# G in two stages, u of two batches in one tile, and v of batch 1 in pieces

## The chip, the cores and the metric

The kernel runs on one core of one Trainium2 chip. The metric is device time in microseconds; the times here are in microseconds unless a unit is named. The engines are PE (TensorE, with its weight loads listed apart as PEld), DVE (VectorE), ACT (ScalarE), POOL (GpSimd) and SP (SyncE, which here only issues transfers). Each works through its own list of instructions in order, and they wait for each other through semaphores.

## The reference

A landmark attention (Nystromformer) over 8 batches, 8 heads, 576 positions and 64 channels is followed by a multiplicative feed-forward layer. All inputs and the output are float32.

```python
q_lm, k_lm = means of q and k over 18 neighbouring positions      # 32 landmarks
A  = softmax(q @ k_lm.T / 8)      # 576 x 32
Bm = softmax(q_lm @ k_lm.T / 8)   # 32 x 32
C  = softmax(q_lm @ k.T / 8)      # 32 x 576
Z  = Bm.T / (norm(Bm, 1) * norm(Bm, inf) + 1e-6)
for _ in range(6):
    Z = 2 * Z - Z @ Bm @ Z
x  = A @ Z @ C @ v                # heads side by side: 4608 x 512
out = ((x @ w1) * (x @ w2)) @ w3 @ w_out
```

## The kernel before

The kernel never forms x. For each batch it makes `zt`, the 32 rows of Z @ C @ v of each head, multiplies them by w1 and w2 into `g` (tile `gt`), and has x @ w1 as `ahat` times `g`, where `ahat` holds the normalised A of four heads. w3 @ w_out is multiplied out once, at the start, into `w34`.

*Start (the fold).* The generator `fold` yields 64 products (L507, three matmuls each) that make `w34`; `turn` transposes blocks of w3 on PE ahead of them (L494). A row of w34 is summed in the PSUM tile `acc` and emptied by ACT (L510). The attention of batch 0 is interleaved with it: a loop over n takes one step of the attention and then one or two products.

*Attention.* The generator `attention` yields after each stage. In order: landmarks `lm` from `parts` (L201, L206) and `qbd`; Bm (psB, L217, then exponent and row sums); the scores C0 and C1 of four heads each (L242, exponent `ect` on ACT, presums on POOL, L253 and on); psR and A0 (L306, L292, exponent `eat`), A1 with the first product C @ v (L323, L328), the second product; six iterations it0 to it5 (L387), with the softmax denominators of A (L349) behind it1; psZ (L407), `zt` in two halves by ACT (L412) and DVE (L413), and `normalise(0)` (L371 on PE, `ahat` on DVE, L374); then `normalise(1)` and G. G has four blocks: two halves of the 1024 columns, each for w1 and w2. A block is 16 matmuls of 64x32 tiles (L430), and is emptied by ACT for w1 (L434) and by DVE for w2 (L436). They are called G00, G01, G10 and G11 here, by column half and matrix.

*Batches.* A loop over b runs the feed-forward part of batch b and, between its matmuls, the attention of batch b + 1. The up phase has 8 units j; each makes 128 columns of both products, 288 + 288 positions: `up(st, j, 0)` is four matmuls (L444) that ACT empties into `a_sb` (L448), `up(st, j, 1)` is four more that DVE multiplies with `a_sb` into `ab` (L450), this is u. Between the two stands one stage of the attention. Then the down phase multiplies `ab` by `w34` in chunks of 128 positions (L464), each in two halves of four matmuls; after each half comes one stage. ACT empties a chunk into `o_sb` (L470) and SP writes it out. As 576 is four and a half chunks, an odd batch begins with a split chunk: 64 positions of the batch before and 64 of its own, in eight 64-wide matmuls for each half. So even batches have 8 halves and odd ones 10. In an even batch two stages follow half n = 6.

At the end of a batch the first stage (L201, `lm`) of the attention after next is run, so that it begins ahead of the up phase.

*PSUM.* Three tiles `big` of two banks are shared by up, C, A, the iterations, the denominators (kept from it1 until `rmix`), normalise, G and every second chunk of down. `acc` and `small` are one bank each.

*Transfers.* POOL issues q and k, as one transfer per tensor (`load_qk`) or as pieces (`qk_pieces`, advanced from inside `landmarks`). SP issues v, the DMA transposes of q and k (`turn_all`, L106), w3, and the output. `load_v_piece` has ACT copy one element into the destination first, so that the transfer waits for ACT's place in its list; `load_v` has no such copy. The order on each engine is the one written in the program.

Of the kernel before, what the change touches and what calls it, by code (L numbers as in the profile page):

```python
# [8 lines left out]
FP16 = mybir.dt.float16  # L9
# [6 lines left out]
S = 576  # L16
# [9 lines left out]
NP = 96  # L26
# [5 lines left out]
def kernel(  # L32
# [42 lines left out]
    def load_v(st, b):  # L75
        vt = st["vt"] if "vt" in st else pin.tile([128, H, 384], FP32, name="vt")
        nc.sync.dma_start(out=vt[0:NP], in_=v[b].rearrange("h (p r) d -> p h (r d)", p=NP))
        st["vt"] = vt
# [117 lines left out]
    def attention(st, bank=None):  # L196
# [225 lines left out]
        for n in range(2):  # L422
            for w in range(2):
                psG = big()
                fs = slice(512 * n, 512 * n + 512)
                for i in range(2):
                    for h in range(4):
                        for qd in range(2):
                            rs = slice(64 * qd, 64 * qd + 64)
                            nc.tensor.matmul(psG[32 * h:32 * h + 32, qd, :], zt[rs, i, h, :],  # L430
                                             wup[rs, h, w, fs], start=(i == 0), stop=(i == 1),
                                             tile_position=(64 * qd, 32 * h))
                if w == 0:
                    nc.scalar.activation(out=g[:, :, w, fs], in_=psG, func=AXF.Copy, scale=1.0 / ZS)  # L434
                else:
                    nc.vector.tensor_scalar(out=g[:, :, w, fs], in0=psG, scalar1=1.0 / ZS,  # L436
                                            scalar2=None, op0=ALU.mult)
                yield

    def up(st, j, w):  # L440
        p = big()
        for qd in range(2):
            for c in range(2):
                nc.tensor.matmul(p[:, c, 0:HS], st["g"][:, qd, w, 128 * j:128 * j + 128],  # L444
                                 st["ahat"][qd][:, c, :], start=(qd == 0), stop=(qd == 1))
        if w == 0:
            st["a_sb"] = po.tile([128, 2, HS], FP16, name="a_sb", bufs=2)
            nc.scalar.copy(out=st["a_sb"], in_=p[:, :, 0:HS])  # L448
        else:
            nc.vector.tensor_tensor(  # L450
                out=st["ab"][:, j, :].rearrange("p (c s) -> p c s", c=2),
                in0=st["a_sb"], in1=p[:, :, 0:HS], op=ALU.mult)


    rows = out.rearrange("(b p g) f -> b g p f", b=B, g=6)

    def down(srcs, half, hold, bank):
        if half == 0:
            hold["ps"] = bank()
        pso = hold["ps"]  # L460
        for j in range(4 * half, 4 * half + 4):
            o = 0
            for _, ab, s0, sz in srcs:
                nc.tensor.matmul(pso[o:o + sz, :], ab[:, j, s0:s0 + sz], w34[:, j, :],  # L464
                                 start=(j == 0), stop=(j == 7),
                                 tile_position=(0, o))
                o += sz
        if half == 1:
            o_sb = po.tile([128, DM], FP32, name="o_sb")
            nc.scalar.activation(out=o_sb, in_=pso[:, :], func=AXF.Copy,  # L470
                                 scale=1.0 / (X64 * X64))
            o = 0
            for b, _, s0, sz in srcs:
                while sz:
                    gi, p0 = divmod(s0, NP)
                    n = min(sz, NP - p0)
                    nc.sync.dma_start(out=rows[b, 2 * (gi % 3) + gi // 3, p0:p0 + n, :],
                                      in_=o_sb[o:o + n, :])
                    o, s0, sz = o + n, s0 + n, sz - n


    def fold(pf, wof, w3f, wsp, warm_up):
# [58 lines left out]
    with tc.tile_pool(name="pf", bufs=2) as pf:  # L541
        wof, w3f = {}, {}
        wsp = pf.tile([128, 2, 8, DM], FP16, name="wsp", bufs=1)

        def load_w3(j, cc=None, eng=nc.sync):
            if j not in w3f:
                w3f[j] = pf.tile([128, DF], FP32, name="w3f", bufs=3)
            sl = slice(0, DF) if cc is None else slice(512 * cc, 512 * cc + 512)
            eng.dma_start(out=w3f[j][:, sl], in_=moe_w3[128 * j:128 * (j + 1), sl])

        def load_wout(c, eng):
            wof[c] = pf.tile([128, DM], FP32, name="wof", bufs=6)
            eng.dma_start(out=wof[c], in_=moe_w_out[128 * c:128 * c + 128, :])

        load_w3(0, 0)
        load_wout(0, nc.scalar)
        load_wout(1, nc.sync)
        load_w3(1, 0, nc.scalar)
        load_wout(2, nc.sync)
        load_wout(3, nc.scalar)  # L560
        load_w3(0, 1)
        load_wout(4, nc.scalar)
        load_w3(1, 1)
        load_wout(5, nc.scalar)

        warm = pf.tile([128, 512], FP16, name="warm", bufs=1)
        nc.vector.memset(warm, 0.0)
        psw = big()

        def warm_up(n):  # L570
            for _ in range(n):
                nc.tensor.matmul(psw[:, 0, :], warm[:, 0:128], warm, start=True, stop=True)

        warm_up(7)

        nc.gpsimd.tensor_copy(out=gate, in_=wof[4][:, 0:1])
        load_qk(sts[0], 0)
        load_qk(sts[1], 1)
        load_weight(0, moe_w1)
        load_weight(1, moe_w2)  # L580
        mask4, par, ones, eye2, iit, onesq, selc, lomask = constants()
        fd = fold(pf, wof, w3f, wsp, warm_up)
        steps(fd, 1)
        load_wout(6, nc.sync)
        load_wout(7, nc.sync)
        load_w3(2)
        steps(fd, 7)
        load_w3(3)
        steps(fd, 8)
        w3f[4] = pf.tile([128, DF], FP32, name="w3f", bufs=3)  # L590
        nc.gpsimd.tensor_copy(out=w3f[4][0:NP, 0:1], in_=sts[0]["qkn"][0:NP, 1, 0, 0:1])
        load_w3(4)
        sts[0]["vt"] = pin.tile([128, H, 384], FP32, name="vt")
        nc.gpsimd.tensor_copy(out=sts[0]["vt"][0:NP, 0, 0:1], in_=sts[0]["qkn"][0:NP, 0, 0, 0:1])
        load_v(sts[0], 0)
        turn_on_pe(sts[0], 1, 0, nc.scalar.copy)
        turn_on_pe(sts[0], 1, 4, nc.vector.tensor_copy)
        landmarks(sts[0], 1)
        steps(fd, 5)
        turn_on_pe(sts[0], 0, 0, nc.scalar.copy)  # L600
        turn_on_pe(sts[0], 0, 4, nc.vector.tensor_copy)
        landmarks(sts[0], 0)
        load_w3(5)
        steps(fd, 4)
        load_w3(6)
        turn_all(1)
        steps(fd, 6)
        at = attention(sts[0])
        for n, m in enumerate((2, 2, 2, 2, 2, 2, 2, 1, 1, 1, 1, 1, 1, 1, 2, 2, 2, 2, 2, 1)):
            steps(at)  # L610
            if n == 1:
                load_w3(7)
                load_v(sts[1], 1)
            elif n == 4:
                landmarks(sts[1], 1)
                load_qk(sts[2], 2)
                landmarks(sts[1], 0)
            steps(fd, m)
        steps(at, 30)
        steps(fd, 64)  # L620
    pab = ctx.enter_context(tc.tile_pool(name="pab", bufs=3))
    at = attention(sts[1], acc)
    steps(at)


    for b in range(B):
        st = sts[b]
        ab = st["ab"] = pab.tile([128, 8, S], FP16, name="ab")
        if b + 2 < B:
            turn_all(b + 2)  # L630
        if b % 2 == 0:
            chunks = [[(b, ab, 128 * t, 128)] for t in range(4)]
        else:
            chunks = [[(b - 1, sts[b - 1]["ab"], 512, 64), (b, ab, 0, 64)]]
            chunks += [[(b, ab, 64 + 128 * t, 128)] for t in range(4)]
        for j in range(8):
            up(st, j, 0)
            steps(at, 1)
            if b + 2 < B and j > 3:
                load_v_piece(sts[b + 2], b + 2, j - 4, st["a_sb"][0:NP, 0, 0:1])  # L640
            up(st, j, 1)
            if b + 2 < B and j == 5:
                pieces = qk_pieces(sts[b + 3], b + 3) if b + 3 < B else iter(())
                landmarks(sts[b + 2], 1, pieces=pieces)
                landmarks(sts[b + 2], 0, pieces=pieces)
        nxt = attention(sts[b + 2], acc) if b + 2 < B else iter(())
        hold = {}
        nd = 2 * len(chunks)
        for n in range(nd):
            bank = (lambda: big()[:, 0, :]) if n // 2 % 2 else acc  # L650
            down(chunks[n // 2], n % 2, hold, bank)
            steps(at, 2 if n == 6 and nd == 8 else 1)
        steps(at, 30)
        steps(nxt)
        at = nxt
# [30 lines left out]
```

## Time and profile before

| What | Value |
|---|---|
| Median of 6 runs | 288.3 |
| Lowest and highest | 287.6 and 290.09 |
| The profiled execution: time | 287.6 |
| Its span in the profile | 285.8 |
| PE busy | 273.9 (96%) |
| DVE, ACT, POOL busy | 167.2, 131.7, 152.1 |
| Batch 0 begins (L201 for batch 1) | 70.75 |
| The next batches begin at | 97.37, 126.37, 153.04, 181.70, 208.37, 237.03 |
| Batch 7 begins (first up) | 263.70 |

The span is from the first to the last instruction of the profile; the time of an execution also holds what lies around it, 1.8 here. A line of the timeline gives the start from the span's beginning, the duration, the engine, the source line, the operation with output and input tiles, their shapes, and how many instructions were merged into it; in brackets is how long the engine was idle before, and what ended that. Rows of adjacent matmuls overlap, because a matmul's end is modelled; the starts do not. "Batch 0 begins" means the place in the order where its up phase starts, with the stage `lm` of the next attention just ahead.

### The profile page before, as it was taken

Reading aid. Unit: us, or ns where it says so; the run is one execution under the profiler, and the core shown is the slowest. Engines: PE = TensorE matmul, PEld = TensorE weight load, DVE = VectorE, ACT = ScalarE, POOL = GpSimd, SP = SyncE. Lnnn points to the kernel's source line nnn. Section 1 sums busy time; section 2 is a strip of 40 time slices with the busy share of each in tenths; the row PEclk is TensorE's granted clock in tenths of the full one; section 3 lists DMA queues with packets and bytes.
Section 4 is the critical chain, followed back from the end, with each engine's and each line's share of the span. In section 5 each row is a group of like instructions: output and inputs, shape, how many; then the busy total and the mean of one; then the engine's idle time right before and its main releaser. Section 6 shows DMA issues by size and latency. Waiting matters only on the chain.

```text
span 285.8 us, 9554 instructions
## 1 busy us (share of the span) xinstructions
PE 273.9 (96%) x4028; PEld 151.0 (53%) x4028; DVE 167.2 (59%) x430; ACT 131.7 (46%) x231; POOL 152.1 (53%) x200
## 2 busy tenths in 40 slices
PE   7999999999999999999999999999999999999994
PEld 3565455444674475437645743474467436744641
DVE  7743243662766666647666775567576646765720
ACT  3653333233752673357336633663375246524531
POOL 1809742980499279906990997099729912400000
PEclk9999999999999999999999999999999999999999
DMA  7999999999149998979789989799998422012124
GB/s 253 296 239 271 248 230 186 237 206 150 32 123 169 191 147 179 182 159 175 185 163 192 163 180 190 135 146 218 184 148 185 125 77 77 2 38 76 37 58 126
DMA packets 61898, 45.57 MB, mean 159 GB/s; under 512 B 35488, under 2 KB 53920, under 8 KB 61856
## 3 DMA queue, kind: packets, MB, share of 16 engines
q1 hardware_dynamic: 47344, 32.12, 47.9%
q0 software_dynamic: 13792, 11.54, 28.6%
q10 hardware_dynamic: 720, 1.31, 1.3%
q8 instruction: 31, 0.51, 0.8%
q14 instruction: 11, 0.09, 0.1%
HBM read 38.80 MB, written 9.44 MB: 169 GB/s over the span
## 4 chain that ended last, share of the span: by engine, by line
PE 73%; DMA 6%; DVE 6%; ACT 6%; POOL 5%; issue 2%; ACTq 1%; DVEq 0%; POOLq 0%
PE big L444 18%; PE acc L464 13%; PE big L464 11%; PE acc L507 8%; PE big L430 6%; DVE ab L450 5%; DMA qkn<-in_q_dram 4%; PE big L387 4%; ACT a_sb L448 3%; PE small L323 2%; DMA wof<-in_moe_w_out_dram 2%; PE acc L323 2%; PE big L371 2%; PE big L242 1%; ACT lm L206 1%
## 5 line engine op out<-in xcount | busy, mean ns | idle before, releaser
L444 PE MATMUL big<-ahat,gt 128*128 128x288 f16 x512 | 74.1, 286 | 2.8 <-ACT a_sb L448 1.7
L450 DVE TENSOR_TENSOR ab<-a_sb,big 128x576 f16<-128x576 f16 x64 | 48.0, 751 | 16.9 <-PE big L444 8.7
L448 ACT CAST a_sb<-big 128x576 f16<-128x576 f32 x64 | 40.9, 639 | 35.9 <-PE big L444 35.1
L444 PEld LDWEIGHTS <-gt 128*128 128x128 f16 x512 | 47.1, 98 | 18.8 <-issue 3.9
L253 POOL TENSOR_TENSOR t<-ect 96x384 f32<-96x384 f32 x16 | 15.9, 994 | 66.4 <-ACT ect L246 65.8
L507 PE MATMUL acc<-wsp,w3t 128*128 128x512 f16 x168 | 41.5, 380 | 0.7 <-ACT w L510 0.7
L464 PEld LDWEIGHTS <-ab 128*128 128x128 f16 (+1 forms) x320 | 24.0, 100 | 32.3 <-issue 9.7
L464 PE MATMUL acc<-w,ab 128*128 128x512 f16 (+1 forms) x192 | 40.9, 382 | 0.0
L464 PE MATMUL big<-w,ab 128*128 128x512 f16 x128 | 32.8, 381 | 0.0
L436 DVE TENSOR_SCALAR gt<-big 128x1024 f16<-128x1024 f32 x16 | 19.6, 1224 | 18.2 <-PE big L430 18.2
L183 POOL TENSOR_TENSOR tr<-qkT 128x768 f32<-128x768 f16 x16 | 26.3, 1644 | 5.1 <-DMA qkT<-qkn 4.9
L507 PEld LDWEIGHTS <-w3t 128*128 128x128 f16 x192 | 17.7, 98 | 20.2 <-issue 3.2
L470 ACT ACTIVATE o_sb<-acc 128x512 f32<-128x512 f32 x20 | 11.9, 597 | 34.3 <-PE acc L464 34.3
L184 POOL TENSOR_TENSOR tr<-tr,qkT 128x768 f32<-128x768 f32 x16 | 26.2, 1640 | 1.3
L500 DVE SCALAR_TENSOR_TENSOR w3t<-big,w3t 128x512 f16<-128x512 f32 x16 | 11.0, 690 | 18.6 <-ACT w3t L499 18.6
L434 ACT ACTIVATE gt<-big 128x1024 f16<-128x1024 f32 x16 | 16.4, 1023 | 7.0 <-PE big L430 7.0
L430 PE MATMUL big<-wup,zt 64*32 64x512 f16 x512 | 19.2, 380 | 0.0
L470 ACT ACTIVATE o_sb<-big 128x512 f32<-128x512 f32 x16 | 9.6, 597 | 20.8 <-PE big L464 20.8
L499 ACT ACTIVATE w3t<-big 128x512 f16<-128x512 f32 x16 | 9.5, 594 | 11.2 <-PE big L494 6.3
L246 ACT ACTIVATE ect<-big 96x768 f32<-96x768 f32 x16 | 12.9, 806 | 3.4 <-PE big L242 2.9
L190 POOL TENSOR_TENSOR o<-o,tr 128x256 f32<-128x256 f32 x16 | 12.9, 804 | 1.3
L374 DVE TENSOR_TENSOR ahat<-eat,big 128x576 f16<-128x576 f16 x16 | 12.0, 749 | 1.4 <-PE big L371 1.4
(310 smaller groups left out, 365.8 us busy)
## 6 DMA issues: line engine op xcount, KB each, us to landing
vt<-in_v_dram SPq DMA_DIRECT2D x24, 288.0 KB, 3.6
out_dram<-o_sb SPq DMA_DIRECT2D x24, 192.0 KB, 3.0
w3f<-in_moe_w_dram SPq DMA_DIRECT2D x6, 512.0 KB, 6.8
out_dram<-o_sb SPq DMA_DIRECT2D x24, 128.0 KB, 3.4
qkn<-in_k_dram POOLq DMA_DIRECT2D x10, 288.0 KB, 5.3
qkn<-in_q_dram POOLq DMA_DIRECT2D x10, 288.0 KB, 5.4
vt<-in_v_dram SPq DMA_DIRECT2D x2, 1152.0 KB, 11.3
wup<-in_moe_w_dram POOLq DMA_DIRECT2D x4, 512.0 KB, 31.1
```

The source lines that it names most:

```text
L183: eng.tensor_tensor(out=tr, in0=x[:, :, 0, :], in1=x[:, :, 1, :], op=ALU.add)
L184: eng.tensor_tensor(out=tr, in0=tr, in1=x[:, :, 2, :], op=ALU.add)
L253: nc.gpsimd.tensor_tensor(out=t3[0:NP], in0=e[:, :, 0:3, :], in1=e[:, :, 3:6, :], op=ALU.add)
L430: nc.tensor.matmul(psG[32 * h:32 * h + 32, qd, :], zt[rs, i, h, :], wup[rs, h, w, fs], start=(i == 0), stop=(i == 1), tile_position=(64 * ...
L434: nc.scalar.activation(out=g[:, :, w, fs], in_=psG, func=AXF.Copy, scale=1.0 / ZS)
L436: nc.vector.tensor_scalar(out=g[:, :, w, fs], in0=psG, scalar1=1.0 / ZS, scalar2=None, op0=ALU.mult)
L444: nc.tensor.matmul(p[:, c, 0:HS], st["g"][:, qd, w, 128 * j:128 * j + 128], st["ahat"][qd][:, c, :], start=(qd == 0), stop=(qd == 1))
L448: nc.scalar.copy(out=st["a_sb"], in_=p[:, :, 0:HS])
L450: nc.vector.tensor_tensor(out=st["ab"][:, j, :].rearrange("p (c s) -> p c s", c=2), in0=st["a_sb"], in1=p[:, :, 0:HS], op=ALU.mult)
L464: nc.tensor.matmul(pso[o:o + sz, :], ab[:, j, s0:s0 + sz], w34[:, j, :], start=(j == 0), stop=(j == 7), tile_position=(0, o))
L470: nc.scalar.activation(out=o_sb, in_=pso[:, :], func=AXF.Copy, scale=1.0 / (X64 * X64))
L507: nc.tensor.matmul(psW[j][:, :], turned[j, c // 4][:, a, c % 4, :], wsp[:, b, c, :], start=(c == 0 and a + b == 0), stop=(c == 7 and a == 1))
```

## The change

Five things are edited.

1. The `yield` behind each block of G moves out of the inner loop, so that G has two stages of two blocks in place of four of one. The extra step after half n = 6 of even batches goes.
2. `ab` becomes one tile of 1152 positions for two batches, with two buffers in place of three tiles of 576. Chunks of 128 run over the pair: four in an even batch, five in an odd one, and none is split.
3. In the up phase unit j = 2 takes no step of the attention, so the stage C1 stands in unit 3 and all later stages one place on.
4. v of batch 1 is loaded in four pieces at n = 4 to 7 of the first loop, each behind a copy by ACT, in place of one transfer at n = 1.
5. q and k of batch 2 are issued in four pieces from inside the landmarks of batch 1.

```diff
                     nc.vector.tensor_scalar(out=g[:, :, w, fs], in0=psG, scalar1=1.0 / ZS,
                                             scalar2=None, op0=ALU.mult)
-                yield
+            yield
...
             nc.vector.tensor_tensor(
-                out=st["ab"][:, j, :].rearrange("p (c s) -> p c s", c=2),
+                out=st["ab"][:, j, st["t0"]:st["t0"] + S].rearrange("p (c s) -> p c s", c=2),
                 in0=st["a_sb"], in1=p[:, :, 0:HS], op=ALU.mult)
...
-    def down(srcs, half, hold, bank):
+    def down(ab, b0, t0, half, hold, bank):
...
         for j in range(4 * half, 4 * half + 4):
-            o = 0
-            for _, ab, s0, sz in srcs:
-                nc.tensor.matmul(pso[o:o + sz, :], ab[:, j, s0:s0 + sz], w34[:, j, :],
-                                 start=(j == 0), stop=(j == 7),
-                                 tile_position=(0, o))
-                o += sz
+            nc.tensor.matmul(pso[:, :], ab[:, j, t0:t0 + 128], w34[:, j, :],
+                             start=(j == 0), stop=(j == 7))
...
             if n == 1:
                 load_w3(7)
-                load_v(sts[1], 1)
             elif n == 4:
-                landmarks(sts[1], 1)
-                load_qk(sts[2], 2)
-                landmarks(sts[1], 0)
+                pieces = qk_pieces(sts[2], 2)
+                landmarks(sts[1], 1, pieces=pieces)
+                landmarks(sts[1], 0, pieces=pieces)
+            if 3 < n < 8:
+                load_v_piece(sts[1], 1, n - 4, ident[0:NP, 0:1])
             steps(fd, m)
...
-    pab = ctx.enter_context(tc.tile_pool(name="pab", bufs=3))
+    pab = ctx.enter_context(tc.tile_pool(name="pab", bufs=2))
...
-        ab = st["ab"] = pab.tile([128, 8, S], FP16, name="ab")
+        if b % 2 == 0:
+            ab = pab.tile([128, 8, 2 * S], FP16, name="ab")
+        st["ab"], st["t0"] = ab, S * (b % 2)
...
-        if b % 2 == 0:
-            chunks = [[(b, ab, 128 * t, 128)] for t in range(4)]
-        else:
-            chunks = [[(b - 1, sts[b - 1]["ab"], 512, 64), (b, ab, 0, 64)]]
-            chunks += [[(b, ab, 64 + 128 * t, 128)] for t in range(4)]
+        chunks = range(0, 512, 128) if b % 2 == 0 else range(512, 2 * S, 128)
         for j in range(8):
             up(st, j, 0)
-            steps(at, 1)
+            steps(at, (1, 1, 0, 1, 1, 1, 1, 1)[j])
...
-            down(chunks[n // 2], n % 2, hold, bank)
-            steps(at, 2 if n == 6 and nd == 8 else 1)
+            down(ab, b - b % 2, chunks[n // 2], n % 2, hold, bank)
+            steps(at)
```

More of the change, by code (lines that the diff above doesn't have):

```diff
@@ L472, in down @@
             o = 0
[L473 to L479, printed above, removed]
+            while o < 128:
+                gi, p0 = divmod((t0 + o) % S, NP)
+                n = min(128 - o, NP - p0)
+                nc.sync.dma_start(out=rows[b0 + (t0 + o) // S, 2 * (gi % 3) + gi // 3, p0:p0 + n, :],
+                                  in_=o_sb[o:o + n, :])
+                o += n
     def fold(pf, wof, w3f, wsp, warm_up):
```

## The prediction

> **What bounds the kernel now.** I read the page's busy rows and clock row first.
>
> ```profile
> PE 273.9 (96%) x4028; PEld 151.0 (53%) x4028; DVE 167.2 (59%) x430; ACT 131.7 (46%) x231; POOL 152.1 (53%) x200
> ...
> PEclk9999999999999999999999999999999999999999
> ```
>
> TensorE (PE) is busy throughout at full clock, and no other engine passes 59%. In this kernel an edit is worth what it does to PE's start times: it takes work off PE, or opens or closes a hole there. Holes sit where PE wants a tile of PSUM that ACT or DVE has not emptied, so I read the timeline of batch 2, PE rows first, at the end of its up phase:
>
> ```profile
> 137.13 1.16 PE L444 MATMUL big<-ahat,gt 128*128 128x288 f16 x8
> 138.22 0.40 PE L387 MATMUL big<-sz__2296,tz__2297 32*32 32x96 f32 x16
> 138.72 1.14 PE L444 MATMUL big<-ahat,gt 128*128 128x288 f16 x8
> 139.79 0.39 PE L387 MATMUL big<-sz__2465,tz__2463 32*32 32x96 f32 x16
> 140.28 0.31 PE L349 MATMUL big<-eat,onesq 128*32 128x144 f16 x8
> 140.58 0.65 PE L444 MATMUL big<-ahat,gt 128*128 128x288 f16 x4
> ```
>
> Durations of adjacent matmul rows overlap, so I cost by differences of starts. Four up matmuls cost 0.49 (140.58 to 141.07, where down begins), eight cost 1.07 to 1.09 where the next rows are in 32-wide tiles: 0.11 for the change. An iteration L387 costs 0.33; the starts at 138.72 and 140.28 lie 0.17 and 0.16 after that, waiting for `ab` to empty a `big`. Then PE, DVE and ACT over the tail of the same batch:
>
> ```profile
> 147.15 0.44 PE L407 MATMUL small<-bmbd,xd 128*64 128x128 f32 x4
> 147.52 0.42 PE L371 MATMUL big<-rmix,selc 128*128 128x144 f16 x4
> 147.78 1.03 PE L464 MATMUL acc<-w,ab 128*128 128x512 f16 x4
> 148.64 0.41 PE L371 MATMUL big<-rmix,selc 128*128 128x144 f16 x4
> 148.99 0.62 PE L430 MATMUL big<-wup,zt 64*32 64x512 f16 x16
> 149.54 1.04 PE L464 MATMUL big<-w,ab 128*128 128x512 f16 x4
> 150.51 1.06 PE L430 MATMUL big<-wup,zt 64*32 64x512 f16 x32
> 151.50 1.04 PE L464 MATMUL big<-w,ab 128*128 128x512 f16 x4
> 152.49 0.62 PE L430 MATMUL big<-wup,zt 64*32 64x512 f16 x16
> 153.04 0.61 PE L201 MATMUL small<-parts,iit 128*128 128x512 f16 x2
> ```
>
> ```profile
> 148.15 0.74 DVE L374 TENSOR_TENSOR ahat<-eat,big 128x576 f16<-128x576 f16 x1
> 149.09 0.76 DVE L374 TENSOR_TENSOR ahat<-eat,big 128x576 f16<-128x576 f16 x1 [0.20 <-PE big L371]
> 151.21 1.22 DVE L436 TENSOR_SCALAR gt<-big 128x1024 f16<-128x1024 f32 x1 [1.36 <-PE big L430]
> ```
>
> ```profile
> 148.84 0.60 ACT L470 ACTIVATE o_sb<-acc 128x512 f32<-128x512 f32 x1 [0.93 <-PE acc L464]
> 149.68 1.02 ACT L434 ACTIVATE gt<-big 128x1024 f16<-128x1024 f32 x1 [0.24 <-PE big L430]
> ```
>
> PE has no hole here. A half chunk of down (L464) takes 0.97 before 32-wide tiles, 0.86 before 128-wide ones. One block of G (L430 x16) takes 0.55 and two together 0.99, so a block not followed by a change of tiles takes 0.43. Emptying one takes ACT 1.02 and DVE 1.22, beginning 0.69 or 0.70 after the block's start. Half chunks between blocks of G hide this today.
>
> **The change, part by part.** I replay PE's starts by these rows; the order of the changed kernel says what each instruction waits for.
>
> *Free unit.* In the seven batches with an attention beside them, unit j = 2 carries no stage, so C1 and all later stages move one unit back and the second iteration with its denominators leaves the up phase for the first gap of down. Its own work (0.33 and 0.31) only moves. Gone are the tile change (1.07 to 0.96, -0.11) and the 0.16 wait at 140.28, since the denominators then find a `big` freed by the first iteration. New: up units 1 to 3 run as sixteen matmuls, and the fourth group needs the `big` that ab(1) empties. In the trace unit 1's second half starts at 129.78 and ab(1) runs 130.54 to 131.30; the fourth group is due at 129.78 + 3 x 0.48 = 131.22 and can start at 131.34: +0.12. Later waits (ab(2), a_sb(3), eat) clear by 0.04 or more. Sum -0.15 per batch, x 7 = -1.05. POOL's second presum and the landmarks behind it come 1.1 later; their last write at 149.92 has 3.1 until L201 at 153.04.
>
> *G in two stages, work on PE.* Batches 0, 2, 4, 6 have 0.55 + 0.99 + 0.55 now, 0.43 + 0.55 twice after: -0.13. Batches 1, 3, 5 have four single blocks of 0.56: -0.28. Together -1.36.
>
> *G in two stages, waits.* Psi (L407) falls one half chunk later, at the end of chunk 2, so ACT's o_sb of that chunk now stands ahead of zt in ACT's queue. Counted from L407: o_sb begins 0.10 (1.06 after its half at 147.78, and this half starts at -0.97) and ends 0.70; zt runs 0.70 to 0.98, where it began at 0.48 (147.63); DVE's half of zt follows; ahat(0) runs 1.22 to 1.96, against 1.00 to 1.74. The three `big` tiles are then chunk 3's, ahat(0)'s and ahat(1)'s. The first block needs ahat(0)'s: due 1.84, starts 2.00 (+0.16). The second needs ahat(1)'s: L371 at 1.49, ahat(1) 1.98 to 2.74, start 2.78 instead of 2.43 (+0.35). So 0.51 per batch, x 7 = +3.57; before, a half chunk of 0.97 stood there. The trace has no such wait; its bounds are 0 (both ahat done in time; a wait can't be a gain) and 0.8 (a whole ahat of 0.75 and its hand-over unhidden). I take 0.51 because every term has a row. The second stage follows: half chunk 3.33, G10 4.30 (its tile, emptied by ACT, free by 3.77), G11 4.73. DVE empties the second block 3.48 to 4.70, so G11 is just free: nothing added, nothing spare.
>
> The Trainium skill, page "TensorEngine Tiling (Array Packing)", section Performance Considerations, PSUM Bottleneck, says that tiling speeds up TensorE but not the emptying of PSUM, which may become the bound; it speaks against putting blocks of G together. If each of the 14 stages ran at DVE's emptying of 1.22 in place of 0.99 on PE, that rule would add an estimated 14 x 0.23 = 3.2, near the 3.57 that I reach through ahat.
>
> *Behind the tail.* Where no down follows (batches 0, 2, 4), ACT must empty G10 (5.11 to 6.13 from L407, after o_sb) before lm, which L201 would allow at 5.94; PE waits for lm: +0.14 to 0.19, I take 0.14 x 3, and 0.05 in batch 6: +0.47. Behind lm stand a_sb(0) and the exponent of B, which PE's 0.29 of waiting there already includes. In odd batches chunk 4 follows the last G, and its two halves now meet without a tile change: -0.11 x 3 = -0.33.
>
> *u in one tile.* The split chunk's eight 64-wide matmuls take 0.98 against 0.97 for four 128-wide ones: pairs already run side by side, so only 0.02 goes, and 0.09 for entering them (0.58 against 0.49 before down): -0.11 x 3, and -0.15 in batch 7: -0.48. The down DMAs keep their pieces. Two buffers of pairs suffice: batch 4 writes what batch 1 finished.
>
> *Fold.* G takes 0.43 + 0.56 twice for four times 0.55 or 0.56 (-0.24), and two tile changes ahead go (-0.22). The last turn of w3 loses a G block as cover for the emptying of `acc`: such an uncovered boundary shows 1.50 from 42.81 to 44.31 where 1.10 is work, +0.40. The first vt copy (0.19 on ACT, from the same copies later) comes ahead of L510 at 43.66, for which PE waits at 44.31: +0.15. The other three fall in ACT's idle time after 46.1. Sum +0.09.
>
> *v and qk in pieces.* SP's transposes hold that queue from 28.78 to 49.99, while the ACT copies are all done by 47, so the four v pieces leave together at 50.8: nothing is paced. One 288 KB piece takes 3.6 to land, the whole 11.3; first use is L323 at 78.69. POOL issues four qk pieces of 0.70 for two of 0.8: landmarks end near 64.7, needed at 70.75. Cost 0; without this cover of 6, POOL's 1.2 would show. In pieces v lands at most 4 x 3.6 - 11.3 = 3 later, which is hidden too. The Trainium skill, page "DMA: Bandwidth & Descriptors", section Rules for kernel authors, would coalesce many small transfers into one.
>
> **Sum.** -1.05 - 1.36 + 3.57 + 0.47 - 0.33 - 0.48 + 0.09 = +0.91. The profiled execution took 287.6 (span 285.8 and 1.8 around it), the fastest of six; 288.5 on its terms. The median of 288.3 is 0.7 above it: 289.2. The measurement of this kernel can tell about 0.5% from no change, 1.44, so below 286.9 is faster and above 289.7 slower.
>
> **Rivals.** *Tail waits don't bind* (0.15): ACT takes zt in time and both ahat finish under the half chunk; then -3.57 falls out and 285.6 remains. For it: DVE is at 59%, and the work on PE does shrink by 3. Against: ahat(1) can't begin before L371, 0.35 ahead of G. *DVE becomes the bound at G11* (0.25): G11 has 0.00 of slack, so each 0.1 that DVE begins the second block's emptying late (behind ahat, at over 0.70 after the block) passes to PE seven times; at 0.3 that is +2.1 and 291.3. For it: 1.22 is the longest step of the tail. Against: after ahat(1) DVE has nothing else queued. It decides from 0.08 per batch on, where the sum of 0.91 reaches 1.44. *The gains and the waits are both about half* (0.10): the free unit and G cancel, 288.3. That v's pacing does nothing is in the forecast already.
>
> **Numbers.** Forecast 0.50, its own range 288.1 to 290.3: of it 0.37 within 0.5% and 0.13 slower. Faster 0.15; same 0.37 + 0.10 = 0.47; slower 0.13 + 0.25 = 0.38. The range takes in forecast, half-way case and the DVE rival up to its price, and leaves most of the first rival out: 286.9 to 291.3.
>
> **What would show it.** Right: L430 in pairs, the second half of the first pair starting 0.7 to 0.8 after the first and waiting for DVE's L374; no wait at L349; batches 2 and 4 about 0.2 longer than 26.67 from L201 to L201, batches 3 and 5 about the 28.66 of now (0.14 less in the tail, 0.14 more at lm). Wrong: L430 pairs running in 0.99 without a wait (then 285.6), or a hole at the fourth block or at lm of over 0.3 (then 291). Also wrong if PE waits for vt or qkT anywhere, or if a hole of over 0.2 stands in units 2 and 3.

## The result and the profile after

The changed kernel takes 289.36 (median of 35 runs), the kernel before, measured beside it, 289.3 (72 runs). The ratio is 1.0005 with a 95% interval of [0.9988, 1.0022]: no change that this measurement can tell. Ratios compare fast executions alone: in some others the records show a lower granted clock and a longer time (292.17 at 0.993 of the full clock here), and of one kernel below five of 12 were of that kind. The profiled execution of the changed kernel took 288.92 with a span of 287.1, against 287.6 and 285.8. Each profile is of one execution, and that of the kernel before was its fastest of six. Line numbers of the changed kernel are a little lower from down on: L462 is the down matmul (L464 before), L466 `o_sb` (L470), L489 `turn` (L494), L502 the product of the fold (L507), L505 its emptying (L510).

The page shows the same picture as before, PE busy throughout at full clock:

```profile
PE 272.5 (95%) x3996; PEld 152.4 (53%) x3996; DVE 167.3 (58%) x430; ACT 130.2 (45%) x235; POOL 153.0 (53%) x202
...
PEclk9999999999999999999999999999999999999999
```

PE has 1.4 less to do and a span 1.3 longer, so holes of about 2.7 are new. To find them I put the starts of L201 of both traces side by side, which cuts the span into batches:

| Stretch | Before | After | Difference |
|---|---|---|---|
| start to batch 0 | 70.75 | 72.47 | +1.72 |
| batches 0, 2, 4, 6 | 26.62, 26.67, 26.67, 26.67 | 26.75, 26.79, 26.80, 26.80 | +0.13 each |
| batch 1 | 29.00 | 28.44 | -0.56 |
| batches 3, 5 | 28.66, 28.66 | 28.44, 28.43 | -0.22 each |
| batch 7 and the end | 22.1 | 22.2 | +0.1 |

The batches together are 0.4 shorter and the start is 1.7 longer. First the batches, by the timeline of batch 2. PE where up ends and down begins:

```profile
140.58 0.39 PE L387 MATMUL big<-sz__2309,tz__2310 32*32 32x96 f32 x16
141.08 0.65 PE L444 MATMUL big<-ahat,gt 128*128 128x288 f16 x4
...
142.52 0.39 PE L387 MATMUL big<-sz__2480,tz__2478 32*32 32x96 f32 x16
142.84 0.31 PE L349 MATMUL big<-eat,onesq 128*32 128x144 f16 x8
```

The denominators (L349) now follow the second iteration by 0.32, without the wait of 0.16, and stand behind the first half of down. Next PE, DVE and ACT in the tail:

```profile
149.17 0.44 PE L407 MATMUL small<-bmbd,xd 128*64 128x128 f32 x4
...
149.81 1.03 PE L462 MATMUL big<-w,ab 128*128 128x512 f16 x4
150.67 0.41 PE L371 MATMUL big<-rmix,selc 128*128 128x144 f16 x4
151.08 0.63 PE L430 MATMUL big<-wup,zt 64*32 64x512 f16 x16
151.93 0.63 PE L430 MATMUL big<-wup,zt 64*32 64x512 f16 x16 [0.22 <-DVE ahat L374]
...
153.45 1.07 PE L430 MATMUL big<-wup,zt 64*32 64x512 f16 x32
154.45 0.61 PE L201 MATMUL small<-parts,iit 128*128 128x512 f16 x2
```

```profile
150.08 0.29 DVE L413 SCALAR_TENSOR_TENSOR zt<-small,zt 128x128 f16<-128x128 f32 x1 [0.79 <-ACT zt L412]
150.28 1.59 DVE L374 TENSOR_TENSOR ahat<-eat,big 128x576 f16<-128x576 f16 x2
```

```profile
149.28 0.60 ACT L466 ACTIVATE o_sb<-acc 128x512 f32<-128x512 f32 x1 [1.94 <-PE acc L462]
149.77 0.27 ACT L412 ACTIVATE zt<-small 128x128 f16<-128x128 f32 x1
...
155.10 0.58 ACT L206 CAST lm<-small 128x512 f16<-128x512 f32 x1
```

The chain of the prediction stands there link by link: `o_sb` at 149.28 ahead of `zt` on ACT, DVE's `zt` at 150.08, both `ahat` from 150.28 to 151.87, and the second block of G 0.85 behind the first where 0.43 is work. The second pair at 153.45 runs in 1.00 without a wait, and `lm` begins 0.65 behind L201, as before (153.04 to 153.69). In the kernel before, `zt` stood ahead of `o_sb` on ACT:

```profile
147.63 0.28 ACT L412 ACTIVATE zt<-small 128x128 f16<-128x128 f32 x1 [1.02 <-PE small L407]
148.84 0.60 ACT L470 ACTIVATE o_sb<-acc 128x512 f32<-128x512 f32 x1 [0.93 <-PE acc L464]
...
153.69 0.58 ACT L206 CAST lm<-small 128x512 f16<-128x512 f32 x1 [0.47 <-PE small L201]
```

The start is another matter. PE in the fold, first before, then after:

```profile
59.51 0.62 PE L430 MATMUL big<-wup,zt 64*32 64x512 f16 x16
60.07 0.82 PE L507 MATMUL acc<-wsp,w3t 128*128 128x512 f16 x3
```

```profile
59.49 1.06 PE L430 MATMUL big<-wup,zt 64*32 64x512 f16 x32
62.33 0.81 PE L502 MATMUL acc<-wsp,w3t 128*128 128x512 f16 x3 [1.78 <-issue]
62.98 0.60 PE L489 MATMUL big<-ident,w3f 128*128 128x128 f32 x4
```

Up to 59.5 the two run level. Then PE stands still for 1.78, and "issue" means that it waited for nothing that the profile shows. In these two profiles this hole is the whole of the start's 1.72. My first reading was the `turn` behind it: SP's transposes of batch 1 ended at 52.20 instead of 49.99, so the last load of w3, `load_w3(7)`, went out 2.2 later.

### The profile page after: what moved, and what is told of

Same layout as the page of the kernel before. It is cut to its first block, busy times and chain, and to the rows that moved or that the text cites. A ratio compares the mean times of both kernels' runs of the same rounds, so it can differ in the third digit from the quotient of the medians.

```text
span 287.1 us, 9505 instructions
## 1 busy us (share of the span) xinstructions
PE 272.5 (95%) x3996; PEld 152.4 (53%) x3996; DVE 167.3 (58%) x430; ACT 130.2 (45%) x235; POOL 153.0 (53%) x202
## 4 chain that ended last, share of the span: by engine, by line
PE 71%; ACT 8%; DMA 6%; DVE 6%; POOL 4%; issue 2%; ACTq 1%; DVEq 0%; POOLq 0%
PE big L444 19%; PE acc L462 13%; PE big L462 10%; PE acc L502 7%; PE big L387 4%; DMA qkn<-in_q_dram 4%; PE big L430 3%; DVE ab L450 3%; PE small L323 2%; DMA wof<-in_moe_w_out_dram 2%; ACT a_sb L448 2%; PE acc L323 2%; DVE ahat L374 2%; PE big L371 2%; PE big L242 2%
## 5 line engine op out<-in xcount | busy, mean ns | idle before, releaser
L502 PE MATMUL acc<-wsp,w3t 128*128 128x512 f16 x168 | 41.4, 379 | 2.8 <-issue 1.8
L462 PE MATMUL acc<-w,ab 128*128 128x512 f16 x160 | 40.3, 381 | 0.0
L462 PEld LDWEIGHTS <-ab 128*128 128x128 f16 x288 | 24.2, 97 | 28.9 <-issue 4.1
L462 PE MATMUL big<-w,ab 128*128 128x512 f16 x128 | 32.7, 381 | 0.0
L466 ACT ACTIVATE o_sb<-acc 128x512 f32<-128x512 f32 x20 | 11.9, 597 | 39.7 <-PE acc L462 39.7
L502 PEld LDWEIGHTS <-w3t 128*128 128x128 f16 x192 | 17.8, 98 | 22.3 <-issue 5.0
L430 PE MATMUL big<-wup,zt 64*32 64x512 f16 x512 | 18.4, 380 | 1.5 <-DVE ahat L374 1.5
L466 ACT ACTIVATE o_sb<-big 128x512 f32<-128x512 f32 x16 | 9.6, 597 | 21.9 <-PE big L462 21.9
L494 ACT ACTIVATE w3t<-big 128x512 f16<-128x512 f32 x16 | 9.5, 594 | 13.2 <-PE big L489 13.1
L208 DVE TENSOR_TENSOR qbd<-lm,par 128x512 f16<-128x512 f16 x8 | 5.5, 688 | 11.8 <-ACT lm L206 11.8
```

What stands on the lines that cost most here:

```text
L462: nc.tensor.matmul(pso[:, :], ab[:, j, t0:t0 + 128], w34[:, j, :], start=(j == 0), stop=(j == 7))
L502: nc.tensor.matmul(psW[j][:, :], turned[j, c // 4][:, a, c % 4, :], wsp[:, b, c, :], start=(c == 0 and a + b == 0), stop=(c == 7 and a == 1))
```

## The experiments

Theory for the batches: the wait at L430 comes from the tile that PE wants next, one that DVE's `ahat` empties late because `zt` stands behind `o_sb` and Psi one half chunk later. Rivals: it comes from the pair of G itself, since two tiles must be emptied in the time of two blocks, or the gain and loss lie in `u` or in the transfers. Theory for the start: w3(7) is late. It fell, as the last experiments show.

**Swapped banks.** Chunks 0 and 2 of down take a `big`, 1 and 3 take `acc`. Then the half chunk between the two L371 no longer takes the `big` that the second block of G needs.

```diff
-            bank = (lambda: big()[:, 0, :]) if n // 2 % 2 else acc
+            bank = acc if n // 2 % 2 else (lambda: big()[:, 0, :])
```

> The changed kernel with the PSUM tiles of down exchanged: chunks 0, 2 and 4 in a big tile, chunks 1 and 3 in acc. Nothing else differs. During the first stage of G the third big is then free, so that its second block needs the tile of ahat(0) and not that of ahat(1). Theory (the waits for ahat eat what the change saves): the hole of 0.42 between the two blocks of the first stage goes in all seven batches, with the 0.07 ahead of the first block. Batches go from 26.8 and 28.4 to about 26.3 and 27.95 from L201 to L201, and the time falls by 3.4, to about 0.988 of before. Rival (the second block waits for something else, or the hole moves to the next bound, DVE emptying the second block before the fourth): batches stay within 0.15 of 26.8 and 28.4, and the time within 0.3% of before.

Measured: 285.49 (6 runs), ratio 0.9893 [0.9868, 0.9917]. Batches 0 to 5 take 26.24, 27.94, 26.30, 27.94, 26.29, 27.94. PE in the same tail:

```profile
149.85 1.06 PE L430 MATMUL big<-wup,zt 64*32 64x512 f16 x32
150.84 1.04 PE L462 MATMUL acc<-w,ab 128*128 128x512 f16 x4
151.81 1.06 PE L430 MATMUL big<-wup,zt 64*32 64x512 f16 x32
```

Both pairs run in 0.99 and every batch is 0.5 shorter: the wait of the tail goes with the choice of bank. DVE still has its 1.22 for each second block, so the pair itself is no bound; the rule of the Trainium skill that the prediction weighed (page "TensorEngine Tiling (Array Packing)", section Performance Considerations), by which the emptying of PSUM may become the bound, does not decide here once another tile is free.

**No free unit.**

```diff
-            steps(at, (1, 1, 0, 1, 1, 1, 1, 1)[j])
+            steps(at, 1)
```

> The changed kernel without the free unit: every unit of up takes one stage again. G's first stage then falls behind the second half of chunk 2, which lies in acc, so a big is free for it, and zt comes ahead of o_sb on ACT. Theory (the free unit gives 0.15 a batch in up and costs 0.49 in the tail): the second block of G starts 0.43 after the first; L349 waits 0.16 again; even batches about 26.4 and odd ones 28.15; time 2.1 to 2.5 under the changed kernel, 0.991 to 0.993 of before. Rival (the free unit is what holds the changed kernel level, as the stages would collide without it): time 0.5 to 1 above before, up phase longer by 0.3 or more.

Measured: 287.84 (12 runs), ratio 0.9966 [0.9939, 0.9993]; batches 26.39, 28.52, 26.44, 28.18, 26.44, 28.18, and no wait at L430. So the batches did what was expected, and the free unit costs 0.25 to 0.36 in each of these but batch 1. The total gained less than expected, and its profile says where: the hole in the fold is there again (1.78 at 63.39), and batch 0 begins at 73.53.

**w3(7) issued by ACT.**

```diff
-                load_w3(7)
+                load_w3(7, eng=nc.scalar)
```

> The changed kernel with the last load of w3 issued by ACT instead of SP at the same place of the program. Theory (the 1.78 hole behind the first stage of G in the fold is the wait of the turn of w3 block 7 for its load, which SP issues late because the transposes of batch 1 hold SP's list until about 50 to 52): the load is issued near 43, no hole stands at that place, batch 0 begins at 70.4 to 70.9 in place of 72.5, batches unchanged; time 0.5 to 1.5 lower, as the hole differs from run to run. Rival (the hole comes from w1 and w2, which the same blocks of G read, or from the issue on PE): the hole stays, batch 0 begins after 71.5.

Measured: 288.85 (12 runs), ratio 0.9996 [0.9969, 1.0023]. The hole behind the pair of G has shrunk from 1.78 to 0.13, but batch 0 begins at 72.07: a hole of 0.48 now stands at 54.07, within a run of L387, none of whose inputs is a load of w3. The total does not move. Half a confirmation, and a first sign that the reading by w3(7) is wrong.

**v and qk whole.** v of batch 1 and q and k of batch 2 are loaded as in the kernel before.

```diff
             if n == 1:
                 load_w3(7)
+                load_v(sts[1], 1)
...
-                pieces = qk_pieces(sts[2], 2)
-                landmarks(sts[1], 1, pieces=pieces)
-                landmarks(sts[1], 0, pieces=pieces)
-            if 3 < n < 8:
-                load_v_piece(sts[1], 1, n - 4, ident[0:NP, 0:1])
+                landmarks(sts[1], 1)
+                load_qk(sts[2], 2)
+                landmarks(sts[1], 0)
```

> The changed kernel with v of batch 1 and q and k of batch 2 loaded as before the change, in whole transfers. Theory (pieces do nothing, all are covered): time within 0.3% of the changed kernel, batches the same within 0.05; batch 0 begins between 70.6 and 73, by when the last load of w3 lands. Rival (the pieces, all behind SP's transposes, make that load later by sharing the DMA engines): no hole in the fold, batch 0 at 70.7, time 1 to 1.5 lower.

Measured: 289.86 (12 runs), ratio 1.0031 [0.9993, 1.0069]; batches 26.74 and 28.44; hole of 2.33 in the fold. Pieces or whole, v leaves SP at 52.8, and no difference can be told.

**Before with u in one tile.** The change's tile of 1152 positions and its `down` (item 2 of the change), in the kernel before, nothing else.

```diff
-        ab = st["ab"] = pab.tile([128, 8, S], FP16, name="ab")
+        if b % 2 == 0:
+            ab = pab.tile([128, 8, 2 * S], FP16, name="ab")
+        st["ab"], st["t0"] = ab, S * (b % 2)
...
-            down(chunks[n // 2], n % 2, hold, bank)
+            down(ab, b - b % 2, chunks[n // 2], n % 2, hold, bank)
```

> The kernel before with u of two batches in one tile and no split chunk, nothing else changed. My sum: odd batches 0.11 shorter (28.55 for 28.66; batch 1 keeps its wait of 0.29 for ab), batch 7 0.15 shorter, even batches 26.6 to 26.7 as before; 0.48 in all, ratio 0.998. Rival: the split chunk hides a wait or was dearer in weight loads, then odd batches are shorter by 0.3 or more and the ratio is 0.995. The order of its fold is that of before, so its profile is a second look at the start: if the late w3(7) of after is chance, batch 0 may begin at 72 or more here too, with a hole ahead of the turn L494; if it is a cost of the changed kernel, batch 0 begins at 70.5 to 71.2.

Measured: 288.36 (12 runs), ratio 0.9967 [0.9936, 0.9997]; even batches 26.62, 26.67, 26.66, odd ones 28.87, 28.52, 28.52. Odd batches are 0.14 shorter. Batch 0 begins at 72.37 with the fold of before, 0.88 of it by two waits of L201 for POOL's `parts` at 34.73 and 35.48, and there is no hole behind G. So the beginning of batch 0 moves by 1.6 from run to run, and 70.75 is at the early end.

**Before with G in two stages.** The two edits of G, in the kernel before.

```diff
-                yield
+            yield
...
-            steps(at, 2 if n == 6 and nd == 8 else 1)
+            steps(at)
```

> The kernel before with G in two stages, and without the extra step after half 6 of even batches; free unit, split chunk and transfers as before. Replay: Psi falls where it did, so ahat(0) is done in time for G00 and a half chunk of down lies between it and ahat(1); the pair G00 and G01 needs no more than ahat(0)'s big and no wait of 0.5 appears. Even batches 0.24 shorter (26.43), odd ones 0.4 to 0.5 shorter (28.2); about 2.2 in all, ratio 0.9925. Rival: the wait belongs to the pair of G itself (two big emptied behind each other, as the emptying rule has it): then each batch has 0.4 to 0.5 of waiting at L430, even batches are 26.8 or more, and the ratio is 1.000 to 1.005.

Measured: 288.75 (12 runs), ratio 0.9955 [0.9918, 0.9992]; batches 26.40, 28.65, 26.45, 28.31, 26.45, 28.32, no wait at L430. The rival that the wait belongs to the pair of G falls: without the free unit the pairs save 0.22 and 0.35 in a batch. But this kernel, in which only G is changed, has the largest hole of all in the fold:

```profile
59.59 1.06 PE L430 MATMUL big<-wup,zt 64*32 64x512 f16 x32
63.80 1.44 PE L507 MATMUL acc<-wsp,w3t 128*128 128x512 f16 x3 [3.15 <-issue]
```

**w3(7) by ACT with swapped banks, and in the kernel before.** The edit of the third experiment, with that of the first, and alone in the kernel before.

```diff
-                load_w3(7)
+                load_w3(7, eng=nc.scalar)
```

> The changed kernel with swapped banks of the down chunks (as in the first experiment) and w3(7) issued by ACT in place of SP. Batches as in the first experiment: 26.25 and 27.95. If the late w3(7) is what the start loses, batch 0 begins at 70.4 to 71.2 for 72.3 and the ratio is 0.984 to 0.986; rival: other transfers of the start set it and take the gain back, then batch 0 begins at 72 and the ratio stays 0.989.

> The kernel before with w3(7) issued by ACT in place of SP, nothing else changed. If before usually gets w3(7) in time and its profile at 70.75 is typical, the ratio is 1.000 and batch 0 begins at 70.5 to 71.2. If the before of most executions waits for w3(7) too, as the changed kernel's profiles do, it gains 0.5 to 1.5, ratio 0.995 to 0.998. Batches 26.67 and 28.66 in both cases.

Measured: 285.27 (6 runs), ratio 0.9856 [0.9811, 0.9901], and 291.9 (12 runs), ratio 1.0017 [0.9974, 1.0060], for before. The first can't be told from swapped banks alone, and its batch 0 begins at 73.64, not at 71. There PE stops 1.57 in the middle of an iteration:

```profile
52.68 0.26 PE L387 MATMUL big<-sz__789,tz__787 32*32 32x96 f32 x1
54.52 0.40 PE L387 MATMUL big<-sz__789,tz__787 32*32 32x96 f32 x15 [1.57 <-issue]
```

Sixteen matmuls of one iteration have all their inputs when the first has run, so neither w3 nor any other tile explains a stop between the first and the second. The second theory for the start came from counting PE's records in order of start: weight loads, matmuls and the waits of its sequencer. In all eight profiles up to here whose fold has such a hole, it ends at record 961 or at record 1217, whatever the kernel: both 193 beyond a multiple of 256. The page has the other half, in its list of DMA queues:

```profile
q8 instruction: 31, 0.51, 0.7%
```

31 packets of 0.51 MB together are 16 KB each, and PE's 3996 + 3996 instructions are a little over 31 times 256. I take it for PE's own code; the profile does not say whose it is. Each hole ends 1.2 to 1.5 after the end of such a packet. The theory: PE asks for its next block of 256 instructions as it enters one, and in the fold the packet queues behind data on the DMA engines. w3(7) falls as cause by the trace too: in the changed kernel it landed 4.7 after 52.20, at 56.9, five before the hole ended.

**Code shifted by 32 instructions.** Sixteen tiny matmuls more, in the changed kernel.

```diff
         warm_up(7)
+        for _ in range(16):
+            nc.tensor.matmul(psw[:, 0, 0:32], warm[:, 0:128], warm[:, 0:32], start=True, stop=True)
```

> The changed kernel with 16 tiny matmuls (32 columns of the warm tile) added to PE's list behind the first warm-up; they compute nothing that is used. They move every later PE instruction 32 places back in PE's list (16 weight loads, 16 matmuls). Theory: the hole of the start is PE waiting for its own code, which arrives in blocks of 256 instructions; in all profiles so far with such a hole it stood at PE record 961 or 1217 (both 193 beyond a multiple of 256). Then a hole, if there is one, comes 32 records earlier in the program: inside the first pair of G, between its 16th and 17th matmul (L430 x16, hole, L430 x16), or 32 records earlier than the sixteen L387 of the third iteration, and PE resumes 1.2 to 1.5 after the end of a 16 KB packet of the instruction queue. Rival, my earlier reading (turn L489 waits for w3(7)): the hole stays where it was, behind the whole pair and ahead of L502 and L489. Batches 26.75 and 28.44.

Measured (one run): 288.26; batch 0 begins at 71.77. PE in the iteration ahead of the denominators:

```profile
52.02 0.38 PE L387 MATMUL big<-sz__779,tz__777 32*32 32x96 f32 x13
52.56 0.35 PE L387 MATMUL big<-sz__779,tz__777 32*32 32x96 f32 x3 [0.16 <-issue]
```

The stop at record 961 has moved about 16 matmuls ahead, from one behind the start of the third iteration into the end of the second, and it ends 1.33 after a packet. It is short (0.16). At record 1217 the pair of G takes 1.10 instead of 0.99, and nothing stands behind it. The place moved as the code theory says and against w3(7); the sizes are those of one execution.

**Late v.** The four v pieces wait for ACT's place at n = 14 to 17, so that v is not on its way when PE asks for the block; in the changed kernel with swapped banks, in the changed kernel, and (the pieces in place of `load_v`) in the kernel before.

```diff
-            if 3 < n < 8:
-                load_v_piece(sts[1], 1, n - 4, ident[0:NP, 0:1])
+            if 13 < n < 18:
+                load_v_piece(sts[1], 1, n - 14, ident[0:NP, 0:1])
```

> The changed kernel with swapped banks, and the four v pieces of batch 1 gated by ACT's place at n = 14 to 17 in place of 4 to 7. Theory: the code block asked for at PE record 961 (near 53.5) queues behind v and w3(7) on the DMA engines, which are full from 52 to 60; without v its packet begins by 57.5 in place of 59.3, PE has it before it reaches record 1217, and the hole of 0.96 behind the first pair of G goes; batch 0 begins near 71.3 for 72.32, the median falls from 285.49 by 0.5 to 1.5, ratio 0.984 to 0.988. v lands by 75, its first use is at 80. Rival: the packet is held up by the transposes or by chance, not by v; then the hole of 1 to 2 stays and the ratio is 0.989 as with swapped banks alone. Batches 26.25 and 27.95 in both.

> The changed kernel with the four v pieces of batch 1 at n = 14 to 17 in place of 4 to 7, nothing else. Theory (code queued behind v): the packet of the instruction queue begins by 57.5, no hole behind the first pair of G, batch 0 begins near 70.7 for 72.47, the median is 1 to 1.7 lower, ratio 0.994 to 0.997. Rival (not v): the hole stays, ratio 1.000 to 1.002. Batches 26.75 and 28.44 in both.

> The kernel before with v of batch 1 in four pieces at n = 14 to 17 in place of the whole at n = 1. Theory: before reaches record 1217 about 1.4 later than the changed kernel (one L507 group and one block of G later), and its packet ended only 1.68 ahead of that in the profile (60.24, PE at 61.92); most of its executions have little or no hole there, so the gain is 0 to 0.8, ratio 0.997 to 1.000, and the packet begins by 57.5 for 58.84. Rival: before usually loses a microsecond or more there too, its profile was a lucky one; then the ratio is 0.996 or lower. Batches 26.67 and 28.66.

Measured: 284.49 (6 runs), ratio 0.9861 [0.9826, 0.9895]; 287.73 (12 runs), 0.9978 [0.9959, 0.9998]; and 288.17 (12 runs), 1.0005 [0.9977, 1.0033]. The trace of each gives the time at which PE reached record 961, where by the theory it asks for the next block, the packet, and when PE went on at record 1217:

| Kernel | G in the fold, v | Record 961 | Packet | Asked to packet | Record 1217 | Hole there |
|---|---|---|---|---|---|---|
| before | four, early | 52.85 | 58.84 to 60.24 | 6.0 | 61.92 | none |
| before, u in one tile | four, early | 54.31 | 60.88 to 62.14 | 6.6 | 63.54 | none |
| after | pairs, early | 52.83 | 59.83 to 61.12 | 7.0 | 62.33 | 1.78 |
| swapped banks | pairs, early | 53.50 | 59.50 to 60.64 | 6.0 | 62.17 | 0.96 |
| no free unit | pairs, early | 53.89 | 60.65 to 61.92 | 6.8 | 63.39 | 1.78 |
| v and qk whole | pairs, early | 52.88 | 60.25 to 61.63 | 7.4 | 62.92 | 2.33 |
| before, G in two stages | pairs, early | 52.94 | 61.35 to 62.56 | 8.4 | 63.80 | 3.15 |
| swapped banks, late v | pairs, late | 54.05 | 57.66 to 58.92 | 3.6 | 61.70 | none |
| after, late v | pairs, late | 55.29 | 58.79 to 60.03 | 3.5 | 62.94 | none |
| before, late v | four, late | 52.95 | 56.53 to 57.45 | 3.6 | 62.02 | none |

With late v the packet comes 3.5 to 3.6 after record 961, with early v 6.0 to 8.4. In the four profiles that the table leaves out, all with early v, it came 5.4 (w3(7) by ACT), 5.0 (that with swapped banks), 6.5 (that in the kernel before) and 5.8 (shifted code) after it. The DMA rows fit a queue. They give the busy tenths of the 16 DMA engines in 40 slices of 54 to 62, in the changed kernel and then with swapped banks and late v:

```profile
DMA  0179967899799999999999999999999999999999
```

```profile
DMA  9999999920589996203000029947699999510000
```

In the first the engines are full from 54.6 to the end, and the packet begins at 59.83, while pieces of v are still landing (58.06 to 62.47). The low digits at 54.0 to 54.4, and at 55.6 to 56.2 in the second row, are no idle time: a row books a packet's whole time in the slice where it begins, and w3(7)'s first packets, most of them 0.8 to 1.0 long, run through those slices. In the second they run nearly empty from 57.2, as w3(7) lands (issued at 53.91, 4.0 to landing), and the packet begins there, at 57.66. Full engines alone do not delay it, though. At record 449 of the changed kernel the packet came 1.3 after PE (39.45 after 38.13), and from 38.0 to 39.5 the engines are just as full: POOL's transfers (q0) take 71.7% of their time and SP's (q1) 38.3%. From 52.8 to 59.9 SP's queue, with w3(7) and v, takes 103.9%. What makes the difference was not tried; that v does delay the packet rests on the runs with late v.

The hole at record 1217 was expected to go, and it goes in both kernels with pairs of G. What was not expected is that both then stop at record 961 instead, by 1.02 and 0.69: that block is asked for at 46.1 and 47.6 and its packet begins 5.2 to 5.7 later, in the stretch of SP's transposes, before v is issued in any of these kernels. So batch 0 begins at 71.86 (71.3 was expected) and at 73.10 (70.7 was expected, and 0.94 of the difference are again waits for POOL's `parts`; this profile is of the slowest of its 12 runs, 289.55, and the changed kernel's own began at 72.47). In the kernel before nothing is gained, as expected. The medians of the two kernels with pairs fell by 1.0 and by some 0.8 (0.27% of 289), against the kernels without late v; their intervals overlap at the edges, so the traces show that the hole at record 1217 goes, and what that is worth in the median is not settled. Swapped banks with late v has the lowest median of the study and, at 0.9861, beats both kernels; from swapped banks with w3(7) by ACT (0.9856) it can't be told.

## Why the prediction was right, point by point

The total was right: 289.2 predicted, 289.36 measured, inside the range, and within 0.5% of before. That the level agrees to 0.2 is luck: the forecast put 0.9 between the two kernels (288.3 and 289.2), but measured side by side the kernel before took 289.3, and the measured difference is 0.1, with an interval of -0.3 to +0.6 that leaves 0.9 out. The split was wrong too. For the batches the steps sum to +0.82, and -0.4 was measured (215.1 from batch 0 to the end, then 214.7); for the fold they give +0.09, and the two profiles differ by +1.72. In the profiles two errors of more than a microsecond nearly cancel, which is luck again.

*Free unit.* Right in size. From the begin of batch 2 to that of its down, 14.70 became 13.90, of which 0.33 and 0.31 only moved: -0.16 where -0.15 was predicted. Not foreseen was batch 1, which had in before a further wait of 0.29 for `ab` at 104.29 that the free unit also removes.

*G, work on PE.* Right: with swapped banks two pairs take 1.98, for the 2.09 and 2.24 of before, so -0.11 and -0.26 where -0.13 and -0.28 were predicted. Pairs alone in the kernel before, another order, give -0.22 and -0.35 in a batch, where that experiment's replay had -0.24 and -0.4 to -0.5.

*G, waits.* The size was right, 0.49 (0.42 and 0.07) for 0.51 (0.35 and 0.16), seven times. The heading was not: with pairs and no free unit there is no wait, with the free unit there is. The half chunk by which Psi moves back, and the bank that the next half chunk takes, make it. Undoing the free unit or swapping the banks each takes it away.

*Behind the tail.* Wrong: 0.47 predicted, nothing measured. ACT began to empty the second pair at 154.15, 4.98 after L407, where the replay had 5.11. `o_sb` was out of its way earlier, so `lm` came 0.65 behind L201 as before. A term worked out as a difference of two times 0.1 apart should have stood at 0 to 0.14.

*u in one tile and chunk halves.* The tile is worth 0.14 in an odd batch for 0.11 predicted. Together with the other terms an odd batch comes to -0.15 - 0.28 + 0.49 - 0.11 - 0.14 = -0.19, with -0.22 measured (terms of the prediction beside measured ones). An even batch comes to -0.16 - 0.13 + 0.49 = +0.20, with +0.13 measured. In batch 7 the stretch from the first up to the last chunk is 0.23 shorter (16.00, then 15.77; 15.77 with the tile alone), for 0.15 predicted.

*Fold.* The failed step: the wait for PE's code was put at nothing. The work itself came out about as summed: from the first G to L201 it is 11.24 before and 11.15 in the changed kernel with late v. But with pairs the second block of G stands where two products of the fold and a turn stood, and PE comes to record 1217 after 7.65 instead of 9.07 from record 961 (with late v, where nothing stops it there). The block is ready at the wait for the packet, its 1.1 to 1.4 and some 1.2 to 1.5 more. In before that was 60.24 + 1.21 = 61.45, and PE came at 61.92: 0.2 to 0.5 spare, which the prediction did not look for, because its views held no wait there. With pairs PE comes 1.4 earlier, so with before's own packet it would have waited an estimated 0.95, and the later packet of the changed kernel's run adds the rest of the hole. The kernel with only G changed (3.15) and the two with late v (none) show both halves. What it takes from the median is best read from late v: some 0.8 in the changed kernel, with the overlap of intervals named above, and none in before. The copies of vt, counted at 0.15, cost nothing: the first ran at 43.49, ahead of L505, and PE went on at 44.31 as before.

*v and qk in pieces.* 0 predicted, and in the medians none can be told. The reason given, that their landing is hidden, is right for v itself, though the 11.3 for the whole was the page's value for two transfers; this one took 9.2, and the last piece landed 2.4 later (62.47 for 60.02). One cost was overlooked: the stretch from the start of the last chunk to the end of the span is 6.12 to 6.18 in the five profiles with v whole and 6.45 to 6.50 in the nine with v in pieces. SP, with three transfers more in its list, waits at the end for the landings in another order. Behind the wait for the last one it then has five more waits of 0.06 each, and none with v whole. What v does to others was not asked: by the late-v runs its 1.15 MB hold up PE's code, whole or in pieces.

*Rivals.* Tail waits that don't bind: fell, the wait is there seven times. DVE as the bound at G11: fell, the second pair runs in 1.00 or 1.01 in each batch. The half-way case has the time nearly right, but neither its gains nor its waits are half of what they were taken for.

## What to carry to other kernels

When a step moves back by one place, follow which buffer the next user of each pool gets: here one half chunk and the order of two banks decided 0.5 per batch, and swapping the banks is free. A start that is crowded with transfers has a hidden customer, the engine's own instructions; a bulk transfer that is needed 20 later can leave after it, and here that took the hole behind G away. A cover with 0.5 to spare in the one profile that one has is not a cover, above all in a stretch whose beginning moves by 1 to 2 between runs.

## What the runs showed of the hardware

As these traces read, PE's code arrives in packets of 16 KB, one for 256 instructions: 31 packets, holes at records 256 apart, and a hole that moved when 32 instructions were added. At record 449 of the changed kernel the packet began 1.3 after PE entered the block, though the engines were full there too, mostly of POOL's transfers. At records 705 and 961 of the fold it took 3.4 to 8.4, and where it came too late PE stood still for up to 3.2 at the next crossing, shown as "issue" idle. The Trainium skill, page "Runtime: NRT & Kernel Launch", section "Instruction fetch mechanics", has the blocks of 256 instructions and the fetch of the next one while the current one runs, and these traces agree; it calls the crossing mostly hidden, which holds in the batches here, where no "issue" hole stands, and not in the fold. Why the packet of record 705 takes so long in the stretch of the transposes (4.1 in the changed kernel, where the DMA rows mostly show under 190 GB/s) was not tried.
